# Attention and a gated two-layer product on one core: loads of the first heads moved ahead, the factor g moved behind a transposition, the order's rules changed

## The chip, the cores and the metric

The kernel runs on one core of one Trainium2 chip. A core has TensorE (PE, matrix products), VectorE (DVE), ScalarE (ACT), GpSimd (POOL) and SyncE (SP, which here only issues transfers); ACT issues transfers too. Each engine works through its own list of instructions in order and waits on semaphores for the others. The metric is the device time of one execution in microseconds (us), lower is better.

## The reference

Eight batches of 12 heads, 448 positions, head size 64, then a layer over all 768 channels:

```python
q_n, k_n = rmsnorm(q, g_q), rmsnorm(k, g_k)          # x / rms(x) * g over the 64
scores = (1/8) * q_n @ k_n^T;  attn = softmax(scores);  a = attn @ v
x = a.transpose(0, 2, 1, 3).reshape(8, 448, 768)
xk = mu_k * x + (1 - mu_k) * x_prev                  # x_prev: the position before
xr = mu_r * x + (1 - mu_r) * x_prev
out = sigmoid(xr @ w_r) * (relu(xk @ w_k)**2 @ w_v)  # w_k 768x1024, w_v 1024x768, w_r 768x768
```

The weights come as 64-bit floats (17 MB in all) and are brought to 32 bits on the chip, by integer operations.

## The kernel before, in words

Every product is made of three passes of 16-bit matmuls over a high and a low half of each operand, so most tiles come in pairs (`wkh`/`wkl`, `vh`/`vl`, the halves of `kk`, `xk`, `xr`).

Attention goes by quads (four heads; index `u`, 24 of them) and pairs (two heads; 48). For a quad, `load` brings k and q, `stats` makes the sums of squares and the reciprocal roots (ACT squares, POOL adds halves, DVE reduces and does three Newton steps), `preps` multiplies, splits into high and low and transposes. For the first three quads (`u < PE_T`) the transposition is done by TensorE (`turn`: products with `ident` into a bank `sc`, then ACT takes the high half and DVE the low half into `stk`); later quads are transposed by transfers. Seven groups of scores per quad (`scores`, six matmuls each, two at a time in 64-row halves of the array) go through `expo` and `probs`: a maximum on DVE, the exponential and its sum on ACT, the split into halves `nat` on ACT and DVE, and a transposing transfer into `pT`. Of the first 21 groups, those in `PE_P` are transposed by TensorE instead (`probs_pe`). `attends` makes the attention product of a pair: 24 matmuls `ot<-pT,vh/vl`, two at a time in 64-column halves, into the one bank `ot`; ACT scales the result into `x`.

The layer: `mixk` and `mixr` blend `x` with the position before (POOL, DVE, ACT, POOL), `moe` makes the products: `mm<-xk,wkh/wkl` (18 matmuls for each of eight column tiles f), `square` (ACT to `kf`, ACT to `kk`, POOL twice; `KF_BUFS` tiles `kf`), then `mm<-wrh/wrl,xr` and `mm<-wvh/wvl,kk`. They use the two banks `mm`. `wload` issues the weights' transfers on ACT's queue, `weights` rebuilds 32-bit values, and `wsplit` finds a scale (products of the tile with itself and with `ones`) and splits; there are 20 weight tiles, 8 of `w_k`, 6 of `w_r`, 6 of `w_v`. The `xk` products of batch 0 wait for the eight `w_k` tiles, all others for all 20.

All of this is written as generators, and `Plan` decides at build time in which order their instructions stand on each engine. It keeps an estimated clock for every engine and picks, again and again, the generator whose next instruction could start first, less a bonus by priority (`PRIO_*`, `BOOST_*`); a TensorE product of attention counts as ready only a margin (`MARGIN`, `MARGIN_A`, `MARGIN_V`, in ns) after its operands by the plan's estimate. On the chip the order is fixed. Every instruction is issued from the one line in `Plan.emit`, so the profile shows one line (L246) for almost all of them, and groups are told apart by tiles. In the first part, tiles `kk` and `xk` (batch 0's homes) are lent out as buffers for weights, k and q, so `xk<-in_k_dram` is a load of the first quad's k and `kk<-in_moe_w_k_dram` a load of weights.

Of the kernel before, what the change touches and what calls it, by code (L numbers as in the profile page):

```python
# [36 lines left out]
NA = 8  # L37
# [5 lines left out]
KF_BUFS = 1  # L43
# [3 lines left out]
PRIO_S = 250  # L47
PRIO_A = 50
PRIO_Q = 100
PRIO_V = 310  # L50
MARGIN = 1200
MARGIN_A = 800
MARGIN_V = 800
# [12 lines left out]
BOOST_Q = 400  # L66
SLACK_S = 3
SLACK_Q = 3
BOOST_V = 0
SLACK_V = 2  # L70
PRIO_W = 100
W_START = 10e3
W_G0 = 0
# [5 lines left out]
PE_P = range(0, 21, 2)  # L79
# [6 lines left out]
DMA_SLOW = 1.0  # L86
PE_SLOW = 1.0
# [95 lines left out]
class Plan:  # L183
    LAT = 35

    def __init__(self, tc):
        self.tc = tc
        self.clk = dict.fromkeys(("PE", "DVE", "ACT", "POOL", "SP"), 0.0)
        self.last, self.use, self.threads = {}, {}, []
        self.form, self.dma_free, self.pool_end, self.n = None, 0.0, 0.0, 0  # L190
# [49 lines left out]
    def emit(self, ops):  # L240
# [7 lines left out]
        if e == "PE":  # L248
            form, cost = ops[0].form
            cost *= PE_SLOW  # L250
            if form != self.form:
                s += 95
# [5 lines left out]
        elif ops[0].fn.__name__.startswith("dma"):  # L258
# [8 lines left out]
            end = max(s + iss, min(self.dma_free - 1200, s + 4000))  # L267
            self.clk[e] = end + 35
            self.dma_free = max(self.dma_free, s + tot - w - 900) + w
            self.note(op, self.dma_free + 900)  # L270
# [11 lines left out]
    def run(self):  # L282
        while self.threads:
            best, key = None, None
            for th in list(self.threads):
# [7 lines left out]
                k = max(self.clk[th[2][0].eng], th[3] + slack) - PS * (th[1]() if callable(th[1]) else th[1])  # L293
# [75 lines left out]
def attn_moe_kernel(tc, q, k, v, g_q, g_k, mu_k, mu_r, w_k, w_v, w_r, out):  # L369
# [21 lines left out]
    G = gq  # L391
    NW = NF + 2 * ND
# [15 lines left out]
    st = {"wdone": 0, "g": 0, "moe": 0, "vl": 0, "gm": False, "mus": False, "want": "xk", "sg": 0, "su": 0, "pu": 0, "vi": 0, "kdone": 0}  # L408
    LD, SS, VF, VV, TQ, PT, BS, BSC, XT, XK, XKN, XR, CNT, OS, CARRY = {}, {}, {}, {}, {}, {}, {}, {}, {}, {}, {}, {}, {}, {}, {}

    plan.st = st

# [59 lines left out]
    def setup():  # L472
        yield SP.dma_start(out=gq, in_=g_q.partition_broadcast(P))
        yield SP.dma_start(out=gk, in_=g_k.partition_broadcast(P))
        yield A.copy(out=ident16, in_=ident)
# [9 lines left out]
        yield V.tensor_scalar(out=G, in0=G, scalar1=gm[:, 1:2], scalar2=None, op0=ALU.mult)  # L485
        yield V.tensor_tensor(out=gm[:, 2:3], in0=gm[:, 1:2], in1=gm[:, 1:2], op=ALU.mult)
# [25 lines left out]
    def load():  # L512
        for u in range(NQ):
# [3 lines left out]
            for n, src in enumerate((k, q)):  # L517
                t = yield from R["qk"].get(u < 3)
                for x in range(2):
                    D = (A if u < LOAD_A and (u or x) else SP).dma_start  # L520
# [17 lines left out]
    def near(u, lim):  # L538
        return BOOST_Q if 7 * u - st["sg"] <= lim else 0

    def stats():
        for u in range(NQ):
# [5 lines left out]
            for n, t in enumerate(LD[u]):  # L548
# [7 lines left out]
                if n == 0:  # L556
# [6 lines left out]
    def preps():  # L563
        for u in range(NQ):
# [23 lines left out]
            TQ[u] = X  # L588

    def turn(t, X, n):  # L590
        tf = t.rearrange("p h c -> p (h c)")
        for a0 in range(0, NT, 4):
            m = min(4, NT - a0)
            z = yield from banks["sc"].get()
            yield [T.transpose(form=("tr", TR_COST * m), out=z[:, a * P:(a + 1) * P], in_=tf[:, (a0 + a) * P:(a0 + a + 1) * P], identity=ident) for a in range(m)]
# [6 lines left out]
            for key, hi, lo in parts:  # L602
# [6 lines left out]
                yield A.copy(out=hi, in_=src)  # L609
# [467 lines left out]
```

## Time and profile before

| what | value |
|---|---|
| three runs | 1082.02, 1082.92, 1084.73 us (median 1082.92) |
| profiled execution | 1082.55 us, of it span 1080.8 us |
| busy in the span | PE 928.3, DVE 801.0, ACT 772.1, POOL 701.1 us |
| first group of scores on PE | 42.76 us |
| first product of the layer on PE | 172.66 us |
| first product that needs all weights | 249.79 us |
| last attention product | 980.69 to 983.10 us |
| transfers | 153.98 MB, mean 142 GB/s |

A PE instruction's busy time overlaps with the next one's, since matmuls are pipelined; what counts is the distance from one start to the next. "Idle before" in a row is the time in which the engine had nothing running before that instruction, with the event that ended it.

### The profile page before, as it was taken

The numbers are of one execution on the slowest core, as the hardware profiler recorded it, in microseconds if no ns is written. First come the engines' busy times: TensorE is split into PE (matmuls) and PEld (weight loads), VectorE is DVE, ScalarE is ACT, GpSimd is POOL, SyncE is SP. The second block draws the span as 40 slices with busy tenths as digits, with TensorE's granted clock in tenths as the row PEclk, the third lists the DMA queues.
The fourth block names the chain that finished last, engine by engine and source line by source line (L and its number), as shares of the span: only waits on it lengthen the run. The fifth ranks groups of instructions, "written<-read, shape, count | busy, mean of one in ns | idle before, by whom it ended". The sixth has DMA issues, their size and how long they took to land. (4 is left out here: it accounts for less than half of the span.)

```text
span 1080.8 us, 19208 instructions
## 1 busy us (share of the span) xinstructions
PE 928.3 (86%) x6150; PEld 487.2 (45%) x6150; DVE 801.0 (74%) x2029; ACT 772.1 (71%) x1789; POOL 701.1 (65%) x729
## 2 busy tenths in 40 slices
PE   1466667738999999999988999999989999999997
PEld 0333333423544555445434545445435554455564
DVE  4879887789888698868887779968987798683000
ACT  3578778767888678878888668877877787783310
POOL 2775597885668675975796557856796658645611
PEclk9967868977999999999999999999999999999999
DMA  8855678884988879868986897789878888762011
GB/s 176 176 121 119 142 149 188 201 169 94 177 153 162 152 152 178 165 135 164 180 172 124 152 166 149 146 162 166 158 141 161 164 162 163 131 111 60 1 30 30
DMA packets 490532, 153.98 MB, mean 142 GB/s; under 512 B 464576, under 2 KB 486848, under 8 KB 490432
## 3 DMA queue, kind: packets, MB, share of 16 engines
q1 hardware_dynamic: 469472, 134.99, 66.4%
q10 hardware_dynamic: 20960, 17.77, 6.0%
q8 instruction: 48, 0.79, 0.3%
q14 instruction: 52, 0.43, 0.1%
HBM read 50.40 MB, written 11.01 MB: 57 GB/s over the span
## 5 line engine op out<-in xcount | busy, mean ns | idle before, releaser
L246 DVE SCALAR_TENSOR_TENSOR nat<-sc,sums,nat 128x448 f16<-128x448 f32 x312 | 203.5, 676 | 42.4 <-ACT nat L246 41.8
L246 PE MATMUL mm<-wvh,kk 128*128 128x384 f16 x896 | 234.1, 326 | 0.5 <-ACT kf L246 0.4
L246 ACT ACTIVATE sc<-sc,sums 128x448 f32<-128x448 f32 x314 | 190.8, 610 | 52.5 <-DVE sums L246 46.5
L246 ACT ACTIVATE nat<-sc,sums 128x448 f16<-128x448 f32 (+1 forms) x328 | 195.7, 645 | 33.1 <-DMA pT<-nat 12.7
L246 PE MATMUL mm<-xk,wkh 128*128 128x448 f16 x768 | 210.3, 356 | 9.3 <-ACT kf L246 7.8
L246 DVE TENSOR_REDUCE sums<-sc 128x1 f32<-128x448 f32 x336 | 194.3, 613 | 17.3 <-PE sc L246 16.9
L246 PE MATMUL mm<-wrh,xr 128*128 128x384 f16 x672 | 179.5, 331 | 0.3 <-ACT o L246 0.3
L246 PEld LDWEIGHTS <-kk 128*128 128x128 f16 (+1 forms) x1362 | 129.2, 98 | 105.8 <-issue 18.8
L246 PE MATMUL sc<-stk 64*128 64x448 f16 (+1 forms) x1152 | 131.8, 374 | 44.3 <-DVE nat L246 29.0
L246 PE MATMUL mm<-wvl,kk 128*128 128x384 f16 x448 | 146.0, 326 | 0.0
L246 PE MATMUL mm<-xk,wkl 128*128 128x448 f16 x384 | 136.3, 355 | 0.0
L246 PEld LDWEIGHTS <-xr 128*128 128x128 f16 x1008 | 96.7, 99 | 79.9 <-issue 20.4
L246 PE MATMUL ot<-pT,vh 128*64 128x448 f16 x768 | 121.2, 370 | 11.3 <-DMA pT<-nat 5.9
L246 DVE SCALAR_TENSOR_TENSOR df<-x,bsc,df 128x448 f32<-128x448 f32 x96 | 107.3, 1128 | 20.2 <-POOL df L246 19.9
L246 PEld LDWEIGHTS <-wkh 128*128 128x128 f16 x768 | 71.4, 98 | 89.4 <-issue 31.9
L246 PE MATMUL mm<-wrl,xr 128*128 128x384 f16 x336 | 111.3, 331 | 0.0
L246 POOL TENSOR_TENSOR qk<-qk,ss 128x896 f32<-128x896 f32 x45 | 77.6, 1725 | 42.2 <-DVE ss L246 28.2
L246 PEld LDWEIGHTS <-stk 64*128 64x128 f16 (+1 forms) x1152 | 42.7, 100 | 120.3 <-issue 85.0
L246 POOL TENSOR_TENSOR nat<-qk,nat 128x896 f16<-128x896 f32 x42 | 80.4, 1914 | 25.2 <-ACT nat L246 21.7
L246 POOL TENSOR_TENSOR kf<-kf 128x448 f32<-128x448 f32 x64 | 64.8, 1013 | 41.2 <-ACT kk L246 40.1
L246 DVE SCALAR_TENSOR_TENSOR o<-o,mm 128x384 f32<-128x384 f32 x56 | 30.6, 546 | 81.1 <-PE mm L246 80.0
L246 POOL TENSOR_TENSOR o<-o,bsc 128x384 f32<-128x384 f32 x48 | 41.8, 870 | 69.1 <-DVE o L246 56.3
(135 smaller groups left out, 1603.7 us busy)
## 6 DMA issues: line engine op xcount, KB each, us to landing
out_dram<-o SPq DMA_DIRECT2D x56, 192.0 KB, 3.4
qk<-in_k_dram SPq DMA_DIRECT2D x42, 224.0 KB, 3.9
qk<-in_q_dram SPq DMA_DIRECT2D x126, 64.0 KB, 2.6
vf<-in_v_dram SPq DMA_DIRECT2D x96, 64.0 KB, 2.9
raw<-in_moe_w_v_dram ACTq DMA_DIRECT2D x12, 512.0 KB, 4.7
vf<-in_v_dram SPq DMA_DIRECT2D x96, 48.0 KB, 2.4
raw<-in_moe_w_r_dram ACTq DMA_DIRECT2D x12, 384.0 KB, 5.0
kk<-in_moe_w_k_dram ACTq DMA_DIRECT2D x8, 384.0 KB, 6.0
```

The source lines that it names most:

```text
L246: r = op.fn(op.kw["out"], op.kw["value"]) if op.fn.__name__ == "memset" else op.fn(**op.kw)
```

## The change

The first quad's k and q are loaded ahead of everything else, half on SP's queue and half on ACT's; weights and v start when the loading of later quads has begun (`LEAD_W`, `LEAD_V`), and their preparation when the first quad is transposed (`GATE_W`, `GATE_V`). For the quads that TensorE transposes, k is no longer multiplied by the factor g (the product of `g_q`, `g_k` and 1/8, normed) before the transposition: behind it the channels lie on the partitions, so g is one column `gc`, by which ACT and DVE scale as they split. The plan keeps a clock for each of two transfer queues instead of one for both, knows which kinds of product share a mode of the array (`MODE`), and adds 600 ns to the start of a product of the other kind while it stands in attention (`SWITCH`), so that attention products come in a row. `kf` gets a second tile, the margins of scores and attention are halved and that of v raised, priorities are changed, the groups of `PE_P` are the odd ones, the weight tiles from the ninth on take a bank `mm` instead of `ot` for their scale, and scores wait while a transposition waits for a bank.

ACT's list of instructions (DMA rows are transfers that it issues), from its start, before:

```order
1 L246 DMA mu<-in_moe_mu_k_dram 128x6x1
2 L246 ACT_TABLE_LOAD
3 L246 CAST ident_75<-ident 128x128
4 L246 DMA mu<-in_moe_mu_r_dram 128x6x1
5 L246 DMA kk_102<-in_moe_w_k_dram 128x3x256 x2
6 L246 DMA xk_103<-in_k_dram 64x7x64
7 L246 DMA raw_126<-in_moe_w_k_dram 128x3x256
8 L246 DMA raw_162<-in_moe_w_k_dram 128x3x256
9 L246 DMA xk_103<-in_k_dram 64x7x64
10 L246 ACTIVATE vh_164,vs<-vf_93 128x512
11 L246 ACTIVATE mm_123<-kk_102 128x384
```

The same place with the change:

```order
1 L258 DMA mu<-in_moe_mu_k_dram 128x6x1
2 L258 DMA gc<-in_g_q_dram 64x1 x2
3 L258 DMA gc<-in_g_k_dram 64x1 x2
4 L258 ACT_TABLE_LOAD
5 L258 CAST ident_75<-ident 128x128
6 L258 DMA mu<-in_moe_mu_r_dram 128x6x1
7 L258 DMA xk_104<-in_k_dram 64x7x64 x2
8 L258 DMA xk_104<-in_q_dram 64x7x64 x2
9 L258 ACTIVATE xk_104<-xk_104 128x896
10 L258 DMA kk_103<-in_moe_w_k_dram 128x3x256 x2
11 L258 DMA raw_182<-in_moe_w_k_dram 128x3x256
```

Four small loads of g and four loads of k and q stand ahead of the first weights, and the squares of k (row 9) ahead of any work on weights or v. DVE's list where its setup ends, before (`vs`, `bstat`, `vl` belong to v, `kk` to a weight tile):

```order
23 L246 RECIPROCAL ismu<-smu 128x2
24 L246 TENSOR_REDUCE vs<-ot_176 128x1
25 L246 TENSOR_SCALAR bstat<-vs 128x1
26 L246 TENSOR_SCALAR bstat<-bstat 128x1 x2
27 L246 SCALAR_TENSOR_TENSOR kk_102<-mm_123,kk_102 128x384
28 L246 SCALAR_TENSOR_TENSOR vl_165<-vf_93,bstat,vh_164 128x512
29 L246 TENSOR_REDUCE vs<-ot_199 128x1
```

The same place with the change (`sst`, `stm`, `ss` are the sums of squares and their roots):

```order
23 L258 RECIPROCAL ismu<-smu 128x2
24 L258 TENSOR_REDUCE sst<-xk_104 128x14
25 L258 TENSOR_REDUCE sst<-nat_185 128x14
26 L258 TENSOR_SCALAR sst<-sst 128x14
27 L258 TENSOR_SCALAR sst<-sst,gm 128x14
28 L258 TENSOR_SCALAR stm<-sst 128x28
```

The statistics of the first quad follow the setup at once; two pairs' v and five weight tiles that stood ahead of them or among them now stand behind the first quad's transposition. PE's list at the ninth attention product, before (an attention product after one of the layer) and with the change (after scores):

```order
1540 L246 MATMUL mm_2633<-wvh,kk_102 128x384
1541 L246 LDWEIGHTS vh_1988
1542 L246 MATMUL ot_2596<-pT,vh_1988 64x448
1543 L246 LDWEIGHTS vh_1988
1544 L246 MATMUL ot_2596<-pT,vh_1988 64x448
```

```order
1622 L258 MATMUL sc_2684<-stk_2409 128x448
1623 L258 LDWEIGHTS vh_2275
1624 L258 MATMUL ot_2634<-pT,vh_2275 64x448
1625 L258 LDWEIGHTS vh_2275
1626 L258 MATMUL ot_2634<-pT,vh_2275 64x448
```

Of the 48 attention products 10 follow scores directly before, and 25 with the change. Counted over PE's whole list, the array goes from one kind (layer, weights and transpositions; scores; attention) to another 345 times before and 326 times with the change. The numbers of matmuls are the same but for 119 transpositions that become 112. The diff, without context lines:

```diff
@@ line 37 of before
-NA = 8
@@ line 43 of before
-KF_BUFS = 1
+KF_BUFS = 2
@@ line 47 of before
-PRIO_S = 250
+PRIO_S = 150
@@ line 49 of before
-PRIO_Q = 100
+PRIO_Q = 50
@@ line 51 of before
-MARGIN = 1200
-MARGIN_A = 800
-MARGIN_V = 800
+MARGIN = 600
+MARGIN_A = 400
+MARGIN_V = 1200
@@ line 66 of before
-BOOST_Q = 400
+BOOST_Q = 600
@@ line 68 of before
-SLACK_Q = 3
+SLACK_Q = 2
@@ line 71 of before
-PRIO_W = 100
+PRIO_W = 200
@@ line 73 of before
-W_G0 = 0
+W_G0 = -9
@@ line 79 of before
-PE_P = range(0, 21, 2)
+SWITCH = 600
+MODE = {"sc": 1, "t6": 2, "av": 3}
+GATE_W = 1
+GATE_V = 1
+W_L1 = 2
+W_L2 = 5
+BOOST_F = 4000
+SLACK_F = 6
+WB_A = 'ot'
+WB_B = 'mm'
+LEAD_V = 1
+LEAD_W = 1
+PE_P = range(1, 21, 2)
@@ line 86 of before
+DMA_SHARE = 1.0
@@ line 190 of before
-        self.form, self.dma_free, self.pool_end, self.n = None, 0.0, 0.0, 0
+        self.form, self.dma_free, self.pool_end, self.n = None, {"SP": 0.0, "ACT": 0.0}, 0.0, 0
@@ line 249 of before
+            form = MODE.get(form, 0)
@@ line 252 of before
-                s += 95
+                s += 105
@@ line 267 of before
-            end = max(s + iss, min(self.dma_free - 1200, s + 4000))
+            other = "ACT" if e == "SP" else "SP"
+            if e == "ACT":
+                end = s + (375 if n > 60000 else 610)
+            else:
+                end = max(s + iss, min(self.dma_free[e] - 1200, s + 4000))
@@ line 269 of before
-            self.dma_free = max(self.dma_free, s + tot - w - 900) + w
-            self.note(op, self.dma_free + 900)
+            begin = max(self.dma_free[e], s + tot - w - 900)
+            both = DMA_SHARE * min(w, max(0.0, self.dma_free[other] - begin))
+            self.dma_free[e] = begin + w + both
+            self.dma_free[other] += both
+            self.note(op, self.dma_free[e] + 900)
@@ line 293 of before
-                k = max(self.clk[th[2][0].eng], th[3] + slack) - PS * (th[1]() if callable(th[1]) else th[1])
+                mode = MODE.get(th[2][0].form[0], 0) if th[2][0].eng == "PE" else None
+                wait = SWITCH if mode == 0 and self.form else 0
+                k = max(self.clk[th[2][0].eng] + wait, th[3] + slack) - PS * (th[1]() if callable(th[1]) else th[1])
@@ line 391 of before
+    gc = const.tile([P, 3], F32, name="gc")
@@ line 408 of before
-    st = {"wdone": 0, "g": 0, "moe": 0, "vl": 0, "gm": False, "mus": False, "want": "xk", "sg": 0, "su": 0, "pu": 0, "vi": 0, "kdone": 0}
+    st = {"wdone": 0, "g": 0, "moe": 0, "vl": 0, "gm": False, "mus": False, "want": "xk", "sg": 0, "su": 0, "pu": 0, "vi": 0, "wkeys": 0, "kdone": 0, "zq": 0, "tq": 0, "lu": 0}
@@ line 412 of before
+    def WB(ci):
+        return WB_A if ci < NF else WB_B
+
@@ line 474 of before
+        for n, g in enumerate((g_q, g_k)):
+            for h in range(2):
+                yield A.dma_start(out=gc[h * HD:(h + 1) * HD, n:n + 1], in_=g.rearrange("(d o) -> d o", o=1))
@@ line 485 of before
+        yield V.scalar_tensor_tensor(out=gc[:, 2:3], in0=gc[:, 0:1], scalar=1.0 / float(HD) ** 0.5, in1=gc[:, 1:2], op0=ALU.mult, op1=ALU.mult)
+        yield V.tensor_scalar(out=gc[:, 2:3], in0=gc[:, 2:3], scalar1=gm[:, 1:2], scalar2=None, op0=ALU.mult)
@@ line 520 of before
-                    D = (A if u < LOAD_A and (u or x) else SP).dma_start
+                    D = (A if (x if u == 0 else u < LOAD_A) else SP).dma_start
@@ line 539 of before
-        return BOOST_Q if 7 * u - st["sg"] <= lim else 0
+        return (BOOST_F if u < 4 else BOOST_Q) if 7 * u - st["sg"] <= (max(lim, SLACK_F) if u < 4 else lim) else 0
@@ line 556 of before
-                if n == 0:
+                if n == 0 and u >= PE_T:
@@ line 588 of before
+            st["tq"] = u + 1
@@ line 593 of before
+            st["zq"] += 1
@@ line 594 of before
+            st["zq"] -= 1
@@ line 609 of before
-                yield A.copy(out=hi, in_=src)
-                yield V.tensor_tensor(out=lo, in0=src, in1=hi, op=ALU.subtract)
+                if n == 0:
+                    yield A.activation(out=hi, in_=src, func=AF.Copy, scale=gc[:, 2:3])
+                    yield V.scalar_tensor_tensor(out=lo, in0=src, scalar=gc[:, 2:3], in1=hi, op0=ALU.mult, op1=ALU.subtract)
+                else:
+                    yield A.copy(out=hi, in_=src)
+                    yield V.tensor_tensor(out=lo, in0=src, in1=hi, op=ALU.subtract)
@@ line 618 of before
-        yield from until(lambda: st.get("vf"))
+        yield from until(lambda: st.get("vf") and st.get("lu", 0) >= LEAD_V)
@@ line 635 of before
-            yield from until(lambda: i in VF)
+            yield from until(lambda: i in VF and st["tq"] >= GATE_V)
@@ line 678 of before
-            yield from until(lambda: u in TQ and len(banks["sc"].free) > (SC_KEEP if gi in PE_P else 1))
+            yield from until(lambda: u in TQ and len(banks["sc"].free) > (SC_KEEP if gi in PE_P else 1) and not st["zq"])
@@ line 766 of before
+            st["zq"] += 1
@@ line 767 of before
+            st["zq"] -= 1
@@ line 865 of before
-                yield from until(lambda: st["g"] >= W_G0 + W_G1 * ci)
+                yield from until(lambda: st["g"] >= W_G0 + W_G1 * ci and st["lu"] >= (LEAD_W if ci < W_L1 else LEAD_W + 1 if ci < W_L2 else LEAD_W + 2))
@@ line 876 of before
-                yield from until(lambda: (ci, i) in RAW)
+                yield from until(lambda: (ci, i) in RAW and st["tq"] >= GATE_W)
@@ line 901 of before
-        pg = yield from banks["ot"].get()
+        pg = yield from banks[WB(ci)].get()
@@ line 905 of before
-        dg = small.tile([P, P], F32, name="dg", bufs=2)
+        dg = small.tile([P, P], F32, name="dg", bufs=1)
@@ line 909 of before
-        banks["ot"].put(pg)
+        banks[WB(ci)].put(pg)
@@ line 922 of before
-        if st["wdone"] == NF:
+        st["wkeys"] += ci < NF
+        if ci < NF and st["wkeys"] == NF:
@@ line 964 of before
-            yield from until(lambda: st.get("rsc") and st["wdone"] >= NA)
+            yield from until(lambda: st.get("rsc"))
```

## The prediction

> **What bounds the kernel now.** I read the busy time by stages first, then what TensorE (PE) waits for, then the timelines of the start.
>
> ```profile
> 0.00:42.76 42.76, 12.74 (x60) 8.41 (x61) 24.73 (x91) 15.08 (x27) 16.78 (x28) 1.00 1.00 194
> 42.76:189.00 146.24, 94.89 (x598) 50.06 (x598) 121.97 (x359) 113.56 (x267) 103.15 (x113) 0.75 0.63 141
> 252.00:324.00 72.00, 69.43 (x485) 36.05 (x484) 61.16 (x163) 60.19 (x145) 42.70 (x45) 0.98 0.83 157
> 324.00:432.00 108.00, 103.82 (x722) 54.62 (x720) 87.54 (x223) 86.68 (x208) 72.45 (x74) 1.00 0.85 161
> 432.00:648.00 216.00, 201.25 (x1369) 102.95 (x1369) 169.26 (x414) 169.90 (x398) 152.77 (x153) 0.99 0.83 158
> 648.00:972.00 324.00, 308.16 (x2093) 157.19 (x2090) 269.29 (x647) 259.06 (x610) 221.22 (x228) 0.99 0.80 151
> ```
>
> The columns are the stage, its length, busy time of PE, weight loads, DVE, ACT and POOL, the granted clock of PE, the share of the transfer engines that is busy, and GB/s. From 252 us on PE is busy in 682.7 of 720 us at a clock of 0.98 to 1.00, while DVE, the next, has 587.3. That stage is PE's: it ends when its products are done, and a product that starts earlier ends the kernel earlier. PE's own loss there is the 37.3 us not busy, and what it loses at changes of kind. Before 252 us PE is not the bound: it is busy in 12.7 of the first 42.8 us and in 94.9 of the next 146.2, at a clock of 0.75. In the first stage the transfer engines are busy all the time (1.00, 194 GB/s), in the second DVE is the fullest (122.0 of 146.2, or 83%).
>
> ```profile
> 24.13 0.61 DVE L246 TENSOR_REDUCE sst<-xk 128x14 f32<-128x448 f32 x1
> 42.76 0.74 PE L246 MATMUL sc<-stk 64*128 64x448 f16 x6
> 248.55 1.30 PE L246 MATMUL sc<-stk 64*128 64x448 f16 x6 [6.23 <-DVE nat L246]
> 249.79 0.50 PE L246 MATMUL mm<-wrh,xr 128*128 128x384 f16 x1
> ```
>
> The statistics of the first quad begin on DVE at 24.1 us, the first scores on PE at 42.8. At 249.8 us PE starts the first product that needs all weights, out of a wait of 6.2 us, and from there it has always something to do. PE's order holds the same work behind that point before and after the change, so the change's time is decided by two things: how early that point comes, and how much PE loses behind it.
>
> **The change part by part.** The sum is made against the profiled execution, 1082.55 us (span 1080.8 and 1.75 around it); the median of the runs, 1082.92, is 0.4 above it.
>
> The first quad ahead: when do the first scores come with the change? Rows of ACT's queue and of the chain from loads to scores:
>
> ```profile
> 0.74 0.48 ACTq L246 DMA_DIRECT2D mu<-in_moe_mu_k_dram  x1
> 1.92 0.40 ACTq L246 DMA_DIRECT2D mu<-in_moe_mu_r_dram  x1
> 4.21 0.62 ACTq L246 DMA_DIRECT2D xk<-in_k_dram  x1
> xk<-in_k_dram ACTq DMA_DIRECT2D x2, 112.0 KB, 6.2
> 19.68 0.54 ACTq L246 DMA_DIRECT2D xk<-in_q_dram  x1
> 21.09 0.93 ACT L246 ACTIVATE xk<-xk 128x896 f32<-128x896 f32 x1
> 22.11 1.12 POOL L246 TENSOR_TENSOR xk<-xk 128x448 f32<-128x448 f32 x1 [6.01 <-ACT xk L246]
> 28.80 0.16 DVE L246 TENSOR_SCALAR sst<-sst 128x14 f32<-128x14 f32 x1
> 33.40 1.09 DVE L246 TENSOR_TENSOR xk<-xk,ss 128x896 f32<-128x896 f32 x1
> ```
>
> ACT issues from 0.74: mu (0.48), four loads of g (each as the second mu, 0.40), mu (0.40), two loads of k (0.62 each), two of q (0.54 each): the last k at 4.5, the last q at 5.6 us. The four loads of g stand in front of them for 1.6 us. A load of k from this queue landed 6.2 us after its issue, so k is there at 10.7 and q close behind it. Squares 0.93, POOL's addition 1.12 for k and 1.12 for q, one reduction 0.61: 14.5. The Newton chain took 4.6 us (28.80 to 33.40) with five weight instructions of DVE in between; alone some 3.3: 17.8. From there to the first scores it took 9.36 us (33.40 to 42.76), about 2 of them weight work in between: 7.4. So first scores at about 25 us, 17.6 earlier.
>
> That isn't the gain, because the weights and v that filled DVE in the meantime come later. Of DVE's 24.73 us before 42.76, what belongs to weights and v is some 15, by tiles:
>
> ```profile
> 0.00:42.76 42.76, 2.80 (x18) 1.91 (x18) 3.85 (x7) 1.67 (x2) 6.01 (x4) 1.00 1.00 194
> 0.00:42.76 42.76, 1.96 (x12) 1.16 (x12) 5.46 (x9) 3.89 (x7) 4.01 (x7) 1.00 1.00 194
> 0.00:42.76 42.76, 0.00 (x0) 0.00 (x0) 1.50 (x2) 1.00 1.00 194
> 0.00:42.76 42.76, 4.06 (x17) 0.94 (x1) 2.67 (x3) 1.00 1.00 194
> L246 DVE TENSOR_TENSOR dg<-ot,ident 128x128 f32<-128x128 f32 x5 | 1.4, 285 | 0.7 <-PE ot L246 0.5
> L246 DVE SCALAR_TENSOR_TENSOR wkl<-kk,WSC,wkh 128x768 f16<-128x768 f32 x1 | 1.1, 1123 | 0.0
> ```
>
> The windows are of tiles `wf` (DVE, the third busy time: 3.85), `kk` (5.46), `vl` (1.50) and `WSC` (4.06, of it `wkl`'s 1.1 is in `kk` too); with `dg` (1.4) it is 15.1. If DVE has to make room for all of it later, the gain is 17.6 - 15.1 = 2.5 us; if all of it falls into gaps, 17.6. DVE has 24 us of gaps in the 146 us that follow, enough in amount, though not each in a useful place. I take 10, in the middle. Below 2.5 it comes if the moved weights are late for the layer's first products, as a rival has it.
>
> The transfers are the same bytes in another order. A rule speaks against a part of this: the Trainium skill, page "DMA: Bandwidth & Descriptors", section "Issuing engines are not separate DMA queues", says that transfers from several issuing engines run on the same 16 engines and only the time to issue is saved. This trace agrees (share 1.00 with two queues issuing, 194 GB/s). By it the split of the first loads over SP and ACT brings nothing beyond issue time; if each queue had its own bandwidth, the first quad's 0.92 MB would come some 2.4 us earlier than at 194 GB/s (4.7 us), and the sum would be lower by at most that.
>
> The factor g: gone are three multiplications, one on DVE and two on POOL:
>
> ```profile
> L246 DVE TENSOR_TENSOR xk<-xk,gq 128x896 f32<-128x896 f32 x1 | 1.1, 1081 | 0.0
> L246 POOL TENSOR_TENSOR qk<-qk,gq 128x896 f32<-128x896 f32 x23 | 49.4, 2147 | 0.1
> L246 DVE TENSOR_TENSOR stk<-sc,stk 128x512 f16<-128x512 f32 x3 | 2.0, 682 | 0.0
> L246 DVE SCALAR_TENSOR_TENSOR nat<-sc,sums,nat 128x448 f16<-128x448 f32 x312 | 203.5, 676 | 42.4 <-ACT nat L246 41.8
> ```
>
> That is 1.1 and 4.3 us. Added are a scale in six splits of k on ACT and DVE: a DVE split with a scale takes 0.676 for 448 columns against 0.682 for 512 without, so at most 0.1 us each, 0.6 in all, and two small operations of 0.16. Bounds: -5.4 if both engines set the pace there, +0.6 if neither did. I take -2 (DVE is the fuller one). The group of scores less that goes through PE's transposition (7 transpositions) lies where PE has idle time; nothing.
>
> A second tile `kf`, and the changes of kind on PE:
>
> ```profile
> L246 PE MATMUL mm<-xk,wkh 128*128 128x448 f16 x768 | 210.3, 356 | 9.3 <-ACT kf L246 7.8
> 499.55 0.33 PE L246 MATMUL mm<-wrl,xr 128*128 128x384 f16 x1
> 499.72 0.33 PE L246 MATMUL mm<-wrh,xr 128*128 128x384 f16 x1
> 499.98 0.74 PE L246 MATMUL sc<-stk 64*128 64x448 f16 x6
> 500.65 0.34 PE L246 MATMUL mm<-wrh,xr 128*128 128x384 f16 x1
> 518.37 0.38 PE L246 MATMUL ot<-pT,vh 128*64 128x448 f16 x2 [1.50 <-DMA pT<-nat]
> 518.56 0.38 PE L246 MATMUL ot<-pT,vl 128*64 128x448 f16 x2
> ```
>
> PE waits 7.8 us in all for ACT to empty a bank into `kf`, since the one tile is held until POOL has read it. With two, between 0 and -7.8; -4, because ACT or POOL may be late for other reasons. Changes: a product of the layer starts 0.17 after the last (499.55, 499.72), but scores start 0.26 after it, so 0.10 for the change; six score matmuls are three pairs at 0.19 (518.37 to 518.56), 0.57, and the layer goes on after 0.67: 0.10 again. 19 changes fewer: -1.9. That "in a row" would mean much is not in the order: 326 changes remain.
>
> Halved margins, other priorities, scale products in a bank `mm`: the plan places scores and attention products closer behind their operands. What PE waits for them now, from 252 to 972 us:
>
> ```profile
> PE ot L246 <- ACT x L246: 8.9, 11, 2.1
> PE sc L246 <- DVE nat L246: 6.7, 13, 1.9
> PE ot L246 <- DMA pT<-nat: 5.9, 7, 1.6
> PE ot L246 <- ACT vh L246: 4.8, 3, 1.8
> ```
>
> Behind a stalled attention product stand the layer's products, which were ready. Bounds: the 37.3 us again if waits double, or -10 if the larger margin of v ends the waits of `ot` on ACT (8.9 + 4.8) and the rest stays. I take +3: a shorter margin leaves less room for errors of the plan, the clock for two queues takes some of them away.
>
> Sum: 1082.55 - 10 - 2 - 4 - 1.9 + 3 = 1067.6; against the median, 1068 us, 1.4% faster. The end is untouched: behind the last attention product only products of the layer stand, in either order.
>
> **The rivals.**
> The start is paid back (0.20): the same bytes have to arrive and the same instructions have to pass through DVE before all weights are done; what attention wins, the weights lose, and the point at 249.8 us stays. For it: transfers at 1.00 until 42.8, and 15.1 of 17.6 us owed on DVE. Against it: after 42.8 us the transfers are at 0.63 and DVE has gaps. It gives 1082.9 - 4 - 1.9, with 1 us for the start, and no change of waits: 1076. The rule of the Trainium skill on issuing engines, above, points this way.
>
> The margins cost more than the start wins (0.15). The point of decision: PE's time not busy behind the first `wr` product, 37.3 us now, grows by more than the 18 us that the other parts bring. If it doubles: 1082.9 - 17.9 + 37.3 = 1102; if it grows by half as much, 1084. For it: 13 waits for a bank of scores and 11 for `ot` already, with twice the margin. Against it: they are short (0.5 and 0.8 us each).
>
> More than I count (0.17): all the moved work falls into gaps (-17.6), `kf` brings 7.8, the waits don't grow: 1082.9 - 17.6 - 5 - 7.8 - 1.9 = 1051.
>
> That the change doesn't do what it says holds for "in a row" alone, which is in the sum as 19 changes.
>
> **How the numbers follow.** My forecast, 1056 to 1075, has 0.48; the payback 1075 to 1084, 0.20; slower for the margins, from 1084, 0.15; more, below 1056, 0.17. Predicted: 1068. The range 1044 to 1088 leaves about 0.08 below and 0.11 above. A measurement of this kernel can tell about 0.3% (3.2 us) from no change: faster (below 1079.7) is 0.48 + 0.17 and 0.11 of the payback, 0.76; within 0.3% the payback's other 0.09 and 0.01 of the margins' case, 0.10; slower the rest of that, 0.14.
>
> **What would show it.** First scores at 25 us (22 to 30), the first `mm<-wrh` near 238 us instead of 249.8, waits of `mm<-xk,wkh` for `kf` near 4 us, PE not busy from there to the last attention product in about 36 to 40 us. Wrong I am at the start if scores come early and the first `wr` product still stands near 250; wrong in the margins if PE's waits for `nat`, `pT` and `x` come to well over 40 us.

## The result, and the profile after

The changed kernel takes 1089.62 us (median of 10 runs, 1087.97 to 1094.49), the kernel before on the same chip 1084.14 (1082.02 to 1087.46): a ratio of 1.0054 (95% interval 1.0037 to 1.0071), 0.5% slower. Forecast were 1068 us and a range of 1044 to 1088. The profiled execution has a span of 1087.4 us, 6.6 more than before.

Both marks that the prediction named came early: the first scores at 27.34 us (forecast 25, before 42.76), the first product that needs all weights at 244.71 (forecast 238, before 249.79). The timeline of PE after:

```profile
27.34 0.93 PE L258 MATMUL sc<-stk 64*128 64x448 f16 x4
181.09 0.90 PE L258 MATMUL mm<-xk,wkh 128*128 128x448 f16 x2 [2.20 <-DVE WSC L258]
244.71 0.32 PE L258 MATMUL mm<-wrh,xr 128*128 128x384 f16 x1
248.12 0.50 PE L258 MATMUL mm<-wrh,xr 128*128 128x384 f16 x2 [1.95 <-POOL xr L258]
250.76 0.50 PE L258 MATMUL mm<-wrh,xr 128*128 128x384 f16 x1 [1.98 <-POOL xr L258]
256.71 1.30 PE L258 MATMUL sc<-stk 64*128 64x448 f16 x6 [5.45 <-DVE nat L258]
```

The second mark misled. Before, PE's last long wait (6.23 us for `nat`) ended at 248.55, ahead of the first `wr` product. In the changed order some `wr` products stand ahead of that wait, which ends at 256.71. From there to the end of the span it is 830.7 us, before 832.2. So the whole loss is there already when PE becomes the bound: 8.2 us later, 1.5 us less behind it. These are single profiles. Two further profiles of each order up to this point (of versions below that differ only later) have the end of the wait at 250.42 and 251.31 in the order before, and at 256.76 and 257.58 in the changed one, so the delay is clear of the scatter and the 1.5 us are not. Between the marks the lead of 15.4 us at the first scores had become 4.4 us of delay at the first attention product (79.28 against 74.88) and 8.4 at the first layer product (181.09 against 172.66).

Windows of before (the first two lines) and after, then after behind 252 us; columns as in the prediction:

```profile
0.00:54.00 54.00, 17.42 (x98) 10.38 (x99) 34.20 (x120) 23.26 (x49) 25.62 (x38) 0.96 0.87 176
54.00:70.00 16.00, 8.94 (x44) 4.91 (x45) 14.72 (x40) 12.56 (x29) 9.59 (x10) 0.61 0.41 84
```

```profile
0.00:54.00 54.00, 19.18 (x100) 12.10 (x100) 35.07 (x120) 23.77 (x51) 16.81 (x28) 1.00 0.72 139
54.00:70.00 16.00, 6.78 (x32) 3.00 (x31) 9.72 (x33) 8.96 (x22) 10.29 (x12) 0.53 0.91 197
60.00:62.00 2.00, 1.51 (x9) 0.42 (x5) 0.00 (x0) 0.00 (x0) 1.73 (x3) 0.50 1.16 224
62.00:64.00 2.00, 0.00 (x0) 0.00 (x0) 0.00 (x0) 0.00 (x0) 0.00 (x0) 0.50 1.08 164
252.00:324.00 72.00, 64.68 (x453) 33.91 (x453) 59.38 (x148) 53.14 (x132) 38.72 (x43) 0.95 0.84 160
324.00:432.00 108.00, 102.12 (x696) 53.49 (x697) 83.30 (x200) 83.28 (x193) 75.13 (x74) 1.00 0.84 152
648.00:972.00 324.00, 306.76 (x2101) 158.77 (x2100) 265.18 (x647) 260.81 (x614) 230.20 (x231) 0.99 0.82 155
```

In 54 us DVE has done the same amount, 34.20 and 35.07 us, only of another kind: the first quad's softmax instead of weights and v. Then it does 5.0 us less in the next 16, and from 62 to 64 no compute engine works at all, while transfers go on (164 GB/s). SP's timeline after shows why (its rows are the issue of transfers, the last one is the longest wait of the queue in the first 70 us: time in all, times, longest):

```profile
24.38 1.21 SPq L258 DMA_DIRECT2D xk<-in_q_dram  x2
46.95 2.58 SPq L258 DMA_DIRECT2D vf<-in_v_dram  x4
49.56 0.61 SPq L258 DMA_DIRECT2D xk<-in_q_dram  x1
50.35 3.66 SPq L258 DMA_TRANSPOSE pT<-xk  x1
54.06 0.58 SPq L258 DMA_DIRECT2D xk<-in_q_dram  x1
54.76 1.26 SPq L258 DMA_DIRECT2D qk<-in_k_dram  x2
56.18 9.08 SPq L258 DMA_DIRECT2D qk<-in_q_dram  x8
SPq L258 <- DVE vl L258: 21.3, 1, 21.3
```

From 25.6 to 46.95 the queue stands at the third pair's v. There are two buffers for v, and what ends the wait is DVE's `vl`, the last step in the preparation of a v, which is now gated behind the first quad. Behind it stand the last loads of quad 2 and all of quad 3, which then come in one crowd with the weights (transfer share 0.91 in 54 to 70, 0.41 before). ACT stands there too, at a weights load of its own:

```profile
63.75 0.37 ACTq L258 DMA_DIRECT2D kk<-in_moe_w_k_dram  x1
64.17 0.51 ACT L258 ACTIVATE mm<-kk 128x384 f32<-128x384 f32 x1 [5.96 <-DMA qk<-in_k_dram]
```

PE's waits after, from 252 to 972 us:

```profile
PE sc L258 <- DVE nat L258: 22.2, 27, 5.5
PE ot L258 <- ACT vh L258: 10.6, 8, 3.0
PE ot L258 <- DMA pT<-nat: 6.5, 8, 1.5
```

In this window the waits for `kf` (6.4 us before) and for `x` (8.9) are gone, and those for `nat` (6.7) and `vh` (4.8) have grown. Of the 22.2 us for `nat`, 5.45 are the last long wait, which lies ahead of 252 us before; without it the growth is 10.0 and 5.8 us, as much as was won. Over the whole span PE's waits for `kf` fall from 7.8 to 2.4 us.

### The profile page after: what moved, and what is told of

Same layout as the page of the kernel before. It is cut to its first block, busy times and chain, and to the rows that moved or that the text cites. A ratio compares the mean times of both kernels' runs of the same rounds, so it can differ in the third digit from the quotient of the medians.

```text
span 1087.4 us, 19104 instructions
## 1 busy us (share of the span) xinstructions
PE 927.5 (85%) x6143; PEld 487.0 (45%) x6143; DVE 806.3 (74%) x2030; ACT 773.2 (71%) x1789; POOL 695.4 (64%) x725
## 5 line engine op out<-in xcount | busy, mean ns | idle before, releaser
L258 DVE SCALAR_TENSOR_TENSOR nat<-sc,sums,nat 128x448 f16<-128x448 f32 x314 | 204.8, 674 | 27.3 <-ACT nat L258 26.7
L258 PE MATMUL mm<-xk,wkh 128*128 128x448 f16 x768 | 214.3, 361 | 6.2 <-DVE WSC L258 3.2
L258 POOL TENSOR_TENSOR qk<-qk,ss 128x896 f32<-128x896 f32 x45 | 77.2, 1716 | 54.4 <-DVE ss L258 38.6
L258 PEld LDWEIGHTS <-wkh 128*128 128x128 f16 x768 | 73.1, 100 | 84.1 <-issue 25.6
L258 POOL TENSOR_TENSOR nat<-nat 128x448 f32<-128x448 f32 x47 | 56.2, 1195 | 50.1 <-ACT nat L258 49.9
```

Source lines behind the costliest of these rows:

```text
L258: r = op.fn(op.kw["out"], op.kw["value"]) if op.fn.__name__ == "memset" else op.fn(**op.kw)
```

## The experiments

For each version the table has the time, the ratio to before with its interval, the DVE busy time in the first 70 us, the end of PE's last long wait for `nat`, and the span from there to the end. (Where a dash stands, the order at that place was another, or there is no wait of 3 us there.) The versions were timed on several chips; the kernel before, timed beside each, had medians of 1082.9 to 1084.4 us, so differences between rows are good to a us or two, and the ratios are the safer measure.

| version | us | ratio | DVE to 70 | last long wait ends | rest |
|---|---|---|---|---|---|
| before | 1084 | 1 | 48.92 | 248.55 | 832.2 |
| changed | 1089.6 | 1.0054 [1.0037, 1.0071] | 44.79 | 256.71 | 830.7 |
| `s_sp` | 1083.7 | 0.9988 [0.9967, 1.0010] | 45.83 | 254.10 | 829.8 |
| `s_flow` | 1083.1 | 1.0001 [0.9978, 1.0024] | 48.62 | 250.07 | 830.4 |
| `s_hold` | 1088.5 | 1.0033 [1.0017, 1.0048] | 46.67 | 257.80 | 828.9 |
| `s_later` | 1088.7 | 1.0057 [1.0037, 1.0078] | 44.24 | 258.16 | 832.2 |
| `s_latest` | 1093.0 | 1.0093 [1.0063, 1.0123] | 41.71 | 258.95 | 830.5 |
| `s_flowlatest` | 1090.9 | 1.0071 [1.0047, 1.0094] | 43.65 | 257.12 | 833.1 |
| `s_newton` | 1076.2 | 0.9923 [0.9897, 0.9949] | 45.29 | 249.21 | 826.3 |
| `s_bnewton` | 1077.9 | 0.9945 [0.9929, 0.9960] | 48.68 | 249.88 | 827.5 |
| `s_flownewton` | 1072.6 | 0.9892 [0.9862, 0.9923] | 48.23 | 246.20 | 832.8 |
| `h_margins` | 1096.6 | 1.0114 [1.0097, 1.0131] | 45.80 | - | - |
| `h_nomode` | 1092.2 | 1.0075 [1.0051, 1.0098] | 46.31 | 256.76 | 829.7 |
| `h_allold` | 1102.8 | 1.0171 [1.0133, 1.0209] | 45.58 | - | - |
| `h_jit` | 1107.6 | 1.0222 [1.0193, 1.0250] | 45.69 | 257.58 | 850.1 |
| `s_blatejit` | 1090.4 | 1.0048 [1.0031, 1.0064] | 48.83 | 251.31 | 834.9 |
| `s_blate` | 1088.8 | 1.0039 [1.0016, 1.0063] | 46.37 | 250.42 | 836.9 |
| `s_nostart` | 1099.6 | 1.0155 [1.0120, 1.0190] | 46.77 | - | - |

A profile shows one execution: that of `s_flownewton`, 1080.75 us, was the longest of its eight and 8.1 us above their median, so its last two columns can't be compared; the others lie within 4 us of their medians.

**The late rules first.** These keep the changed order until the last of the 20 weight tiles is done, and plan the rest by other rules: the margins of before (`h_margins`), no grouping of attention products (`h_nomode`), all late rules of before (`h_allold`), and a change without a meaning (`h_jit`).

```diff
+            MARGIN, MARGIN_A, MARGIN_V = 1200, 800, 800      # h_margins
+            SWITCH = 0      # h_nomode, with every form a mode of its own
+            # h_allold: both, and PRIO_S 250, PRIO_Q 100, BOOST_Q 400, SLACK_Q 3
+            JIT = 1.002     # h_jit: the plan's cost of PE products times JIT
```

> The changed kernel with one rule turned back: from the moment all 20 weight tiles are done, the plan uses the old margins (1200, 800, 800 ns); everything up to there stands in the same order, so the first product with w_r should start near 244.7 us as in the changed kernel. Theory margins: TensorE's 22.2 us of waits for banks of scores (DVE nat) between 252 and 972 us come from the halved margin; turned back they fall to about 7, and the time to about 1078 us. Theory in a row: they come from the 600 ns rule; they stay near 22 and the time near 1089. Theory chance: the time moves by some us in either direction, no more than with a meaningless disturbance of the order.

> The changed kernel with the other rule turned back from the same moment: no 600 ns on products of the other kind, every change of form charged as before. Theory in a row: waits for banks of scores fall from 22.2 to about 7 us, time about 1076 to 1080, although the changes of kind rise by some 20 (2 us). Theory margins: waits stay near 22 us, time 1089 to 1092. Theory chance: as the meaningless disturbance.

> Margins, the 600 ns rule and the priorities of scores and preparation all turned back from the same moment; the start, the second kf tile and the clocks of two queues stay. If the loss behind the first product with w_r is made by these rules, the not-busy time of TensorE from 252 to 972 us falls from 46.6 to the 37.3 of the kernel before or lower (kf no longer waits), and the time to 1076 (5 us earlier start of that stage, 2 to 6 less for kf). If it is not, it stays near 1089.

> A meaningless disturbance: from the same moment the plan takes TensorE's products 0.2% longer than it did, all rules as in the changed kernel. Theories margins and in a row: the time stays at 1089 within 2 us and waits for banks of scores near 22. Theory chance: the order comes out otherwise and the time moves by 3 to 8 us, as much as the rules are said to do.

None of them is faster than the changed kernel. `h_nomode` is within the scatter, 2.6 us above it; the others are clearly slower, the one without a meaning by most, 18 us. PE's waits in it, from 252 to 972 us:

```profile
PE sc L259 <- DVE nat L259: 33.2, 24, 5.5
PE ot L259 <- ACT vh L259: 13.6, 9, 3.6
```

In that stretch PE is not busy for 58.7 us, against 46.6 in the changed kernel, and its granted clock is 0.97 against 0.99, so not all of the 18 us need be waits. Taking back the margins or the grouping did not bring the loss back in any of these orders. More can't be said, since the time of one order of the late part says little of a rule: orders planned almost alike lie up to 18 us apart. On the kernel before, the same disturbance, and all of the changed late rules on its start:

> The kernel before, its order kept until the last of the 20 weight tiles is done, and from there planned with TensorE's costs 1.002 times as long: a meaningless disturbance. Its twin on the changed kernel gave 1107.6 us against 1089.6. Theory 'chance of the order': before is one draw too and a good one; this draw lies above 1084 by 5 to 25 us (1089 to 1109). Theory 'the changed start costs it': before's late part has slack that the changed one lacks, so this stays at 1084 within 4.

> The kernel before until the last of the 20 weight tiles is done, and from there the changed kernel's rules (halved margins, products of one kind in a row, the new priorities). With the changed kernel's start, its own rules gave 1089.6 and the old ones 1102.8. Theory 'the start costs it': start as before (some 4790 matmuls left at 324 us), so 1080 to 1086 us, on the level of before or under. Theory 'chance of the order': anywhere from 1084 to 1105 us, with the matmuls left at 324 us as before and the loss after it.

Both come out above before, by 5.9 and 4.6 us: before has the better order of the three, and the changed rules brought no better one. The scatter is smaller than on the changed start (2.6 to 18 us), and two draws are few; that before's order is good by chance is not shown. The attempt to undo the change's start by its constants gave another order altogether:

```diff
-GATE_W, GATE_V, LEAD_V, LEAD_W, BOOST_F, SLACK_F = 1, 1, 1, 1, 4000, 6
+GATE_W, GATE_V, LEAD_V, LEAD_W, BOOST_F, SLACK_F = 0, 0, 0, -9, 600, 2
```

> The changed kernel with the part on the start undone: v and weights are no longer held behind the first quads (both gates off, the leads of the loads back, the early priority back to 600 and 2 quads); factor g, the cost of a change of kind, the margins and the two queues stay. Theory 'the start costs it': 4785 to 4805 matmuls left at 324 us (4819 in the changed kernel, 4788 before), the first scores at 35 to 45 us, and 1080 to 1086 us unless the order behind 324 us is a bad draw. Theory 'it is the rules or the order': 4815 to 4835 left, 1088 or more.

Its first scores came at 56.3 us, later than in either kernel, and 4826 matmuls were left at 324 us (4819 changed, 4788 before). It is not the start of before, and does not tell whether the changed start costs the time. From here on the order was kept fixed, and single transfers were moved.

**SP's queue.** `s_sp` moves the third pair's v loads nine SP instructions back; `s_flow` also the first transposition by DMA, by three. `s_hold` moves the weights load at which ACT stood eight ACT instructions back. All engines' other lists stay as they are.

```diff
-                    yield SP.dma_start(out=vf[...], in_=src[h][:, t::2, :])
+                    d = SP.dma_start(out=vf[...], in_=src[h][:, t::2, :])
+                    d.hold = 9 if i == 2 else 0     # s_sp, s_flow
+            d.hold = 3 if u == 0 and x == 0 and t0 == 0 else 0   # s_flow: transposition
```

> The changed kernel with one thing moved: the loads of the third pair of v heads stand nine instructions later in SyncE's queue, so that quad 2's last q loads, one DMA transposition and quad 3's loads no longer stand behind them; every other engine's list is word for word the same. In the changed kernel SyncE's queue stands at that v load from 25.6 to 46.95 us. Theory 'blocked queue' (the late second and third quads' loads cost the time): quad 3's loads issue some 8 us earlier, the stretch 60 to 64 us in which all engines stand is gone, VectorE is busy 13 to 15 us of 54 to 70 us (9.7 in the changed kernel), the third attention product starts 4 us or more before 121.7 us, and the time is 1084 to 1086 us. Theory 'the start is paid back on VectorE' (the same work, in a row on an engine that has no gap to give): the gap only moves, and the time is 1089 us within 2. Theory 'chance of the order' (the plan's own order after 250 us sets the time): the order is fixed here, so also 1089 within 3.

> The changed kernel with one thing moved: the 13th load of the weights (tile 6, first half), which ScalarE issues, stands eight instructions later in ScalarE's list; all other engines keep their lists. In the changed kernel ScalarE stood 6.0 us at this load, until quad 3's k load on SyncE's queue, which had the same completion semaphore, had landed. Theory 'lane stall': ScalarE's wait of 6.0 us at 57 to 64 us is gone or under 1.5 us, the stretch 60 to 64 us has work in it, the first wr product that PE does without waiting comes 3 to 5 us earlier, and the time is 1085 to 1087 us. Theory 'paid back on VectorE': quad 3's data land no earlier and VectorE has nothing else to do, so the wait only moves to it, the time is 1089 within 2.

> As the run that moved the third pair's v loads nine instructions back on SyncE, and also the first transposition by DMA (of the attention weights of quad 0) behind three further SyncE instructions, so that quad 3's two k loads wait for nothing but their buffer, which PE frees at about 46 us. All other engines keep the changed kernel's lists. Theory 'blocked queue': quad 3's k loads issue at 46 to 48 us (53.2 in the run with the v loads alone, 54.8 in the changed kernel), the empty stretch about 60 to 64 us shrinks by 3 us or more, fewer matmuls are left at 324 us than the 4810 of that run, and the time is 1079 to 1082 us. Theory 'VectorE sets the pace': the loads come earlier and nothing else does, 1083.7 within 2.

`s_sp` gave 5.9 us back, though not all its signs came: the queue then stood at the transposition, quad 3's k loads issued at 53.18, 1.6 us earlier and not 8, DVE was busy for 10.7 us from 54 to 70 and not 13 to 15, and the empty stretch only shrank. In `s_flow` quad 3's k issues early and the stretch is filled; SP, two windows and PE's last long wait:

```profile
46.99 1.26 SPq L256 DMA_DIRECT2D qk<-in_k_dram  x2
49.70 1.43 SPq L256 DMA_TRANSPOSE pT<-xk  x1
60.00:62.00 2.00, 1.77 (x12) 0.73 (x8) 1.85 (x6) 0.34 (x1) 1.82 (x3) 0.50 1.17 284
62.00:64.00 2.00, 1.33 (x6) 0.90 (x8) 1.70 (x8) 2.00 (x6) 1.83 (x4) 0.50 0.79 184
250.07 1.30 PE L256 MATMUL sc<-stk 64*128 64x448 f16 x6 [5.45 <-DVE nat L256]
```

Quad 3's k issues at 46.99 instead of 54.76, DVE works through the stretch that was empty, and PE's last long wait ends 6.6 us earlier. The time goes back by 6.5 us, to that of before and not the 1079 to 1082 expected; between `s_sp` and `s_flow` no difference in the time can be measured, though in their profiles the last long wait ends 4 us apart. `s_hold` did not do what it was for: ACT stood 4.63 us, until 63.44, at another of its weights loads, behind quad 3's q, and its time can't be told from that of the changed kernel. `s_flow` shortened ACT's stand as well, to 1.71 us; in `s_sp`, with the same time, it was still 4.66. What ACT's stand alone costs is open.

**The first quad.** If the queue is cured and the first scores come 15 us earlier than before, why is nothing won? These put its loads back behind others, all else fixed: SP's half behind the eight loads of v (`s_later`); also ACT's half behind the first four loads of weights, which pass the small loads of the gains (`s_latest`); and the latter on `s_flow` (`s_flowlatest`).

```diff
+            d.first = u == 0 and n == 0 and x == 0 and h == 0
+            # from here on, instructions are collected until the loads of v (and weights)
+            # are planned; those are issued first, the others behind them in their order
```

> The changed kernel with the first quad's four loads on SyncE put back behind the eight loads of v that stood behind them, and nothing else moved: the other engines' lists are word for word the same. The first scores come some 6 to 7 us later (33 to 35 us, 27.3 in the changed kernel, 42.8 before). Theory 'first quad on the path' (the step of the prediction that gave 10 us of gain for 17.6 us): a loss of 4 to 7 us, 1094 to 1097 us, and first xr product as much later. Theory 'paid back' (by 252 us the same products are done however early the first scores come): under 2 us, 1088 to 1092 us, the first xr product within 2 us of 244.7.

> The changed kernel with the loads of the first quad put back behind other data on both queues: behind the eight loads of v on SyncE and behind the first four loads of weights on ScalarE (which also pass the small loads of the gains); every other instruction on every engine stands where it stood. In the run that moved SyncE's half alone the first scores came only 1.9 us later (29.2), since ScalarE's half was the later one, and the first xr product came 1.9 us later too. Here the first scores come 8 to 12 us later (35 to 40 us). Theory 'first quad on the path of the changed order': the first xr product at 252 to 257 us (244.7) and 1096 to 1101 us. Theory 'paid back behind it': first xr product at 245 to 248 us and 1089 to 1092 us.

> The same delay of the first quad's loads on the version with SyncE's queue cured (1083.1 us, first xr product at 238.5). Theory 'first quad on the path': 8 to 12 us later throughout, 1091 to 1095 us. Theory 'paid back': the cured queue leaves the first quad some slack before the next quads, 1083 to 1086 us and the first xr product at 239 to 241 us.

The first half moved the first scores by 1.9 us only, and the time by nothing that can be told. The whole moved them by 6.3 and 6.4 us (33.59 and 33.73), less than the 8 to 12 expected. It cost 3.4 us on the changed kernel, half of the delay and only just clear of the scatter, and 7.8 on the cured one, all of it. So the first quad's loads are on the path of the cured order, and in part on that of the changed one. DVE's account suggests how; windows of the first 70 us of before, changed, `s_flow`, `s_latest`, `s_flowlatest`:

```profile
0.00:70.00 70.00, 26.36 (x141) 15.29 (x142) 48.92 (x159) 35.82 (x77) 35.22 (x47) 0.88 0.76 155
```

```profile
0.00:70.00 70.00, 25.96 (x130) 15.10 (x131) 44.79 (x152) 32.73 (x73) 27.09 (x39) 0.89 0.76 152
```

```profile
0.00:70.00 70.00, 28.12 (x140) 16.88 (x140) 48.62 (x162) 36.74 (x82) 30.82 (x43) 0.90 0.81 167
```

```profile
0.00:70.00 70.00, 23.66 (x120) 13.88 (x120) 41.71 (x141) 28.92 (x64) 23.95 (x36) 0.96 0.69 140
```

```profile
0.00:70.00 70.00, 24.42 (x124) 14.64 (x126) 43.65 (x147) 30.95 (x69) 25.27 (x38) 0.94 0.68 144
```

In the changed order the first quad is all that DVE has in the beginning; if it is late, DVE stands, and the account at 70 us is 3.1 and 5.0 us lower. In the order before, DVE had weights and v in that time.

The account at 70 us is a sign, not a measure. One order gives 46.4 to 48.9 us in three profiles (before, `s_blatejit`, `s_blate`), the changed one 44.8 to 46.3 in five (with the four `h_`), `s_sp` at 45.8 lies in the range of the changed order and ends its last long wait 2.6 us earlier, and `s_hold` at 46.7 lies above it and ends it later. The account up to the end of the last long wait is steadier. For before, changed, `s_flow`, then `s_bnewton` and `s_newton` (the shorter roots, below):

```profile
0.00:248.55 248.55, 139.83 (x868) 76.66 (x869) 194.12 (x558) 170.35 (x369) 170.63 (x186) 0.81 0.72 157
0.00:256.71 256.71, 144.99 (x873) 77.39 (x874) 202.69 (x562) 170.09 (x369) 162.58 (x180) 0.81 0.73 149
0.00:250.07 250.07, 145.58 (x874) 77.06 (x875) 205.30 (x562) 170.38 (x369) 163.09 (x180) 0.80 0.74 153
0.00:249.88 249.88, 148.00 (x869) 80.32 (x869) 189.82 (x528) 170.84 (x369) 170.29 (x186) 0.78 0.73 156
0.00:249.21 249.21, 146.06 (x873) 77.68 (x874) 196.25 (x532) 169.99 (x369) 162.11 (x180) 0.80 0.77 154
```

Up to that point the changed order has 562 instructions for DVE instead of 558, and they keep it busy for 202.7 us instead of 194.1 (202.7 to 204.3 and 192.6 to 194.1 over three profiles each). It stands idle for 54.0 us against 54.4 (52.4 to 54.0 and 54.4 to 57.8). With the queue cured it stands for 44.8 only: the early start does fill some 10 us of DVE's gaps, and the changed order has as much more for DVE to do ahead of the same point. Three more `nat` and two more `df` are part of it, and the `vl` take 1.07 us each instead of 0.82; why they take longer is not known.

**DVE's length.** Two of three refining steps of the reciprocal root are left out for every quad but the first (138 instructions less; the roots are coarser, the rest is computed as it was), in the changed kernel's order, in that of before, and in that of `s_flow`.

```diff
+                op.skip = skip and it > 0     # skip=u > 0; planned as before, not issued
```

> The changed kernel in the same planned order, with two of the three refining steps of the reciprocal root left out for every quad but the first (138 VectorE instructions fewer, 1.46 us a quad; the roots are coarser, the rest is computed as before). Theory 'VectorE sets the pace of the start, what was done early is owed later': VectorE has about 10 us less to do before PE is saturated, the first wr products run 6 to 10 us earlier and the time is 1078 to 1083 us. Theory 'blocked queues' (VectorE stands for loads anyway): under 3 us of gain, 1086 to 1090 us. Theory 'chance of the order, PE waits for the softmax late': the waits for VectorE in 252 to 972 us (22.2 us for nat) shrink by a half, time 1080 to 1085, with 60 to 64 us still empty.

> The kernel before, in its own order, with the same 138 VectorE instructions left out (two of three refining steps of the roots for every quad but the first). On the changed kernel this gave 1076.2 against 1089.6, 13 us, with 43 fewer matmuls left at 324 us. Theory 'VectorE sets the pace of the start in both kernels': the same 8 to 13 us here, 1071 to 1076 us, and the changed kernel stays behind. Theory 'VectorE became the pace only with the changed start (before it was the loads)': under 5 us, 1079 to 1085 us.

> The changed kernel with both cures: the queue order of the run that moved the third v pair and the first transposition on SyncE, and the two refining steps of the roots left out for all quads but the first. Alone they gave 1083.1 and 1076.2 us (1089.6 unaltered); the kernel before with the shorter roots gave 1077.9. Theory 'blocked queue and VectorE's pace are two causes': they add up, 1068 to 1072 us. Theory 'one cause' (a shorter VectorE list only helped because it freed what SyncE's queue stood at): 1075 to 1078 us, on the level of the shorter roots alone and of before with them.

13.4 us on the changed order, 10.5 on the cured one (1083.1 to 1072.6), 6.3 on the order before. In the profiles of the changed order 7.5 us of it are there at the end of the last long wait and 4.4 behind it; DVE had 6.4 us less to do up to there. Before, it had 4.3 us less and stood idle for 5.6 more: the wait ended no earlier (249.88) and 4.7 us came behind it, so there the forecast of 8 to 13 us was too much. DVE does not set that point before, as it does with the change. The two cures together gave 17 us of a sum of 6.5 and 13.4, and 1072.6 lies between the 1068 to 1072 of two causes and the 1075 to 1078 of one, much nearer to the first: two causes that overlap a little. With the shorter roots the cured order beats that of before (1072.6 against 1077.9); with the full ones they are level. It is the fastest version here, 1.1% faster than before, at the price of coarser roots.

## Why the prediction was wrong

- **First quad ahead, -10: the step that failed.** The first half was right: first scores at 27.3 (25 forecast), and with the queue cured their time is on the path. Wrong was that the moved weights and v would fall into gaps of DVE for half their amount and bring the point at 249.8 us forward by 10. By 54 us DVE had done 35.07 us of work against 34.20: the 15 us were still owed, as the bound of 2.5 us had it. Up to the end of the last long wait the changed order has some 9 us more for DVE, which takes back the 10 us of gaps that are filled when the queue is cured. That wait then ends at 250.07 (248.55 in the kernel before), and the whole change is at a ratio of 1.0001 (0.9978 to 1.0024): nothing is won. The shorter roots show that DVE sets this point. It is not shown that the early start alone, without the other rules of the start, brings nothing, since undoing it gave another order. Of the rivals, "the start is paid back" comes nearest; its 1076 counted on gains of the other parts that did not show, and it did not have the queue.
- **Left out: SP's queue.** The prediction moved v behind the first quad and never asked what stands behind v's loads. The third pair's v stood 21 us for its buffer, with quad 2's and 3's loads behind it. That costs 5.9 to 6.5 us (`s_sp`, `s_flow`), and turns "no gain" into "slower".
- **The marks.** "First `wr` product near 238" could not tell: it came 5 us earlier while the bound came 8.2 us later, since the order around it had changed. In `s_flow` it came at 238.49, just as forecast, and nothing was won. PE's time not busy up to the last attention product is 51.9 us from the first `wr` product, 42.5 from the end of the last long wait (36 to 40 forecast, 37.3 before). The sign of wrong margins did not come: the waits for `nat`, `pT` and `x` from 252 to 972 us are 28.7 us together, not well over 40.
- **Factor g, -2:** not tried alone. POOL has done 8.8 us less by 54 us, but only one multiplication of 2.1 us in that is the factor's; work on weights, which comes later, is some 10 us less. No run says that the factor brought time.
- **`kf`, -4; fewer changes, -1.9; margins, +3:** their sum of -2.9 stands against -1.5 behind the last long wait, less than executions of one kernel differ by (1082.02 to 1087.46 us before). The mechanism was right for `kf` (7.8 us to 2.4, with waits near 4 forecast). That waits would grow was right as well, but more than allowed for: those for `nat`, `vh`, `x` and `pT` from 252 us on, without the last long wait, went from 26.3 to 33.9 us, 7.6 where +3 was forecast. The price of a change was not measured again; its 0.19 us for a pair of scores was read from a pair of attention. That the three are real effects of rules, and not the luck of one order, the runs don't show: orders with other rules, or with a nudge, lie 2.6 to 18 us higher.
- **"Margins cost more than the start wins"** has the right sign for another reason: its point of decision, more than 18 us of added time not busy, was not reached (5 us from the end of the last long wait), and the one order with the old margins takes 1096.6 us, more.

## What to carry to other kernels

Before counting a lead at the start as a gain, add up what the fullest engine has to do up to the point where the next bound begins, in both orders: if the sum has not become smaller by then and the gaps have not been filled, the lead is only a swap. Then walk down each in-order queue that the moved work passes, and ask of every transfer when its buffer becomes free and what stands behind it. Judge a planner's rule by several orders, a meaningless nudge among them, and compare PE's last long wait rather than the first product of some kind.

## What was not expected

ACT stood 5.96 us at a load that it issues itself, released by a transfer of SP's queue (quad 3's k): in the program, that load and quad 3's k use the same completion semaphore, and the load waits until the k has counted on it, so the two queues are not independent of each other. A change of 0.2% in one cost of the plan moved the kernel by 18 us, more than three times what the whole change did.
